# Two blocks of a feed-forward layer share one PSUM bank, and weight steps may be issued while the tensor engine waits

## The chip, the cores and the metric

The kernel runs on one core of a Trainium2 chip. Time is device time in microseconds (us) of the whole launch, as the median of several runs. Engines are named as the profile names them: PE is the tensor engine (PEld its loading of stationary operands), DVE the vector engine, ACT the scalar engine, POOL the GpSimd engine, SP the queue that issues most transfers.

## The reference

```python
# attention: q, k, v are (8, 8, 576, 64); 64-wide blocks, a query sees its own block and earlier ones
scores = scale * np.matmul(q, k.transpose(0, 1, 3, 2))
mask = block_i >= block_j
attn = softmax(np.where(mask, scores, -1e9))
x = (attn @ v).transpose(0, 2, 1, 3).reshape(8, 576, 512)
# Fourier mixing and a feed-forward net
mixed = np.real(np.fft.fft(np.fft.fft(x, axis=1), axis=2))
u = x + mixed
un = (u - mean(u)) / np.sqrt(var(u) + 1e-6)             # per row of 512
ch = np.maximum(un @ w_ch1, 0.0) @ w_ch2                 # 512 -> 2048 -> 512
return u + ch
```

## The kernel before

There are 64 heads (8 batches of 8). The heads run as attention with exact maxima: `max_part` (line 392 reduces), `shift`, `scores` (two exponentials on ACT, lines 434 and 435, and a difference `pl` on POOL, line 436), `values` (matmuls into `av`). Each operand is held as a high and a low part. After eight heads of a batch, `fourier_steps` reads the batch back mirrored (`mirror`: two plain loads by SP and three gathers by POOL, line 538), folds it on DVE (lines 549 and 550), and multiplies it with cosine and sine tables (`stage1`, `stage2_sin`, `stage2_cos`). `normalized_steps` normalizes 256 rows (`norm`, line 694) and transposes them on PE (`turn`, line 705 casts, line 706 takes the low part). Each such group of 256 rows becomes one feed; there are 18 feeds.

A feed (`feed_steps`) has 16 blocks f of 128 hidden columns. `first(f, part)` issues 3 of the 12 matmuls (256 columns each) that build a block in a PSUM tile `h`; behind the last part ACT writes `gh` = relu of it (line 743) and DVE the rest `gl` (line 744). `second(f, n)` issues 3 of the 6 matmuls (512 columns each) that multiply `gh` and `gl` with the second weights into the two tiles `acc`. The order is first(0), first(1), second(0), first(2), second(1), and so on. The pool `h` has two banks; each tile is a bank, of which a block fills half.

What stands where is set by a planner in the program itself. Lanes (loads, preparation, v, maxima, scores, values, transforms) hold steps with estimated costs, `after` (keys that must be done in the estimate) and `need` (keys that must have been issued). The loop at the end of the kernel issues the ready step of the lowest `place`; feed steps are the filler, issued where no lane is ready. A further stream, the weight steps (`weight_lane`: `weight_single` packs the 64-bit weights of the input with three DVE operations, lines 823 to 825, and squares them on ACT, line 826; `weight_parts` makes the two fp16 parts on ACT, lines 850 and 853, and on POOL, line 854, or DVE, line 856), is the `side`. A side step was issued only if it was ready at the estimated present:

```python
if side is not None and may(side) and ready(side) <= now:
    engine, cost = side.chain[0]
    ahead = queues[engine].fit(max(now, ready(side)), cost) - now
```

PE keeps the program's order. On the other engines a scheduler places instructions as their operands allow, and each engine then works strictly through its own list.

Of the kernel before, what the change touches and what calls it, by code (L numbers as in the profile page):

```python
# [9 lines left out]
F32 = mybir.dt.float32  # L10
F32R = mybir.dt.float32r
F16 = mybir.dt.float16
# [7 lines left out]
B, H, S, D = 8, 8, 576, 64  # L20
DM = H * D
FF = 4 * DM
P = 128
NF = FF // P
NK = DM // P
# [10 lines left out]
AHEAD = (1.5, 6.0)  # L36
FREE = 0.5
# [141 lines left out]
def tile_attn_fourier_ffn(  # L179
# [5 lines left out]
    work = pool("work")  # L185
    ps_av = pool("ps_av", 1, space=PSUM)
    ps = {name: pool(name, n, space=PSUM) for name, n in BANKS.items()}
# [5 lines left out]
    def mm(*args, **kw):  # L193
        return tc.keep_in_program_order(nc.tensor.matmul(*args, **kw))  # L194
# [43 lines left out]
    for at in range(0, NCOS, P):  # L238
        w = min(P, NCOS - at)
        nc.vector.tensor_scalar(ZT[:, at:at + w], ones[0:34, 0:w], 0.0, None, op0=ALU.mult)  # L240

    W = const.tile([P, 2 * NF + 2, 2, DM], F16, name="W")
# [4 lines left out]
    now = 0.0  # L247
    queues = {x: Queue() for x in "DAGQ"}
# [5 lines left out]
    def may(step):  # L254
        return all(x in done for x in step.after) and all(x in done for x in step.need)

    def ready(step):
        r = max((done[x] for x in step.after), default=0.0)
        return max(r, min(rings[x][0] for x in lent)) if step.bank else r

    def issue(step):
        nonlocal current, now
        t = max(now, ready(step))
        if step.cost:
            now = t = t + step.cost
            for x in queues.values():
                x.forget(now)
        free = None
        for engine, cost in step.chain:
            if engine == "B":  # L270
                free = t + HOP
            else:
                t = t + cost if engine == "L" else queues[engine].book(t + HOP, cost)
        t += HOP
        if step.key is not None:
            done[step.key] = t
        if step.bank:
            current = min(lent, key=lambda x: rings[x][0])
            rings[current] = rings[current][1:] + [t if free is None else free]
        step.emit()  # L280
# [444 lines left out]
    def feed_steps(me, uh, ul, us, stores):  # L725
        acc = []
        gs = {}

        def first(f, part):
            fs = slice(P * (f % NK), P * (f % NK + 1))  # L730
            if part == 0:
                gs[f] = ps["h"].tile([P, 512], F32, name="h")[:, 0:2 * P]
            t = gs[f]
            i = 3 * part
            for w, x_ in ((0, uh), (0, ul), (1, uh)):
                mm(t, W[:, NK * (f // NK) + part, w, fs], x_[:, part], start=(i == 0), stop=(i == 3 * NK - 1))
                i += 1
            if part < NK - 1:
                return
            gh = work.tile([P, 2 * P], F16, name="gh", bufs=3)  # L740
            gl = work.tile([P, 2 * P], F16, name="gl", bufs=3)
            gs[f] = gh, gl
            nc.scalar.activation(gh, t, AF.Relu)  # L743
            nc.vector.scalar_tensor_tensor(gl, t, 0.0, gh, op0=ALU.max, op1=ALU.subtract)  # L744

        def second(f, n):
            if f == 0:
                acc.append(ps["acc"].tile([P, DM], F32, name="acc"))
            gh, gl = gs[f]
            ns = slice(P * n, P * (n + 1))  # L750
            for j, (g_, w) in enumerate(((gh, 0), (gh, 1), (gl, 0))):
                mm(acc[n], g_[:, ns], W[:, NF + f, w], start=(f == 0 and j == 0), stop=(f == NF - 1 and j == 2))
            if f == NF - 1:
                u = us[n]
                nc.vector.scalar_tensor_tensor(u, acc[n], inv_w, u, op0=ALU.mult, op1=ALU.add)
                stores[n](u)

        def first_steps(f):
            for part in range(NK):
                last = part == NK - 1  # L760
                after = (("t", me, 0), ("t", me, 1)) + ((("g", me, f - 2),) if f > 1 else ()) if part == 0 else ()
                if me == 1:
                    after += (("w", NK * (f // NK) + part),)
                yield Step(
                    lambda part=part: first(f, part), 0.327, ("A0.4", "D0.44") if last else (), after,
                    ("g", me, f) if last else None,
                )

        def second_steps(f):
            for n in range(2):  # L770
                yield Step(
                    lambda n=n: second(f, n), 0.648, ("D0.76",) if f == NF - 1 else (), (("g", me, f),) + ((("w", NF + f),) if me == 1 else ()),
                    ("F", me) if f == NF - 1 and n == 1 else None,
                )

        yield from first_steps(0)
        for f in range(NF):
            if f + 1 < NF:
                yield from first_steps(f + 1)
            yield from second_steps(f)  # L780


    stage = [utile() for _ in range(3)]
# [74 lines left out]
    def weight_lane():  # L858
        yield Step(lambda: weight_loads(0), 0.0, ("Q5",), (("L", 0),), ("load",))
        def single(x):  # L860
            i, n, at = LANDS[x]
            return Step(
                lambda: weight_single(x), 0.0, (f"D{0.19 + 0.26 * n}", f"D{0.19 + 0.62 * n}", f"D{0.19 + 0.63 * n}", f"A{0.38 + 0.43 * n}"),
                (("load",),), "w32" if x == len(LANDS) - 1 else None,
            )

        def scale(w):
            return Step(lambda: weight_scale(w), 0.1, ("D0.16", "B", "D0.45"), (), ("scale", w), True)

        def parts(i):  # L870
            return Step(lambda: weight_parts(i), 0.0, ("A1.45", "G1.2") if i < NF else ("A0.73", "D0.75"), (("scale", i // NF),), ("w", i))

        for x in range(len(LANDS)):
            i, n, at = LANDS[x]
            yield single(x)
            if i == NF - 2:
                yield scale(0)
            if i >= NF:
                for j in range(n):
                    yield parts(i - NF + j)  # L880
        yield scale(1)
        for i in range(NF):
            yield parts(NF + i)
# [22 lines left out]
    heads = [next(x) for x in lanes]  # L906
    weights, filler = weight_lane(), None
    side = next(weights)
    while True:
        if filler is None and feeds:  # L910
            filler = next(feeds[0], None)
            if filler is None:
                feeds.pop(0)
                continue
        able = [
            i for i, x in enumerate(heads)
            if x is not None and may(x) and (i == len(lanes) - 1 or x.place < H or "w32" in done)
        ]
        if side is not None and may(side) and ready(side) <= now:
            engine, cost = side.chain[0]  # L920
            ahead = queues[engine].fit(max(now, ready(side)), cost) - now
            idle = min((ready(heads[i]) for i in able), default=now)
            if filler is not None and may(filler):
                idle = min(idle, ready(filler))
            if ahead <= AHEAD[engine == "D" and min((heads[i].place for i in able), default=H) >= H] or ahead + cost + FREE <= idle - now:
                issue(side)
                side = next(weights, None)
                continue
        feed = filler is not None and may(filler)
        sure = now - (MARGIN if feed and ready(filler) <= now else 0.0)  # L930
        soon = [i for i in able if ready(heads[i]) <= sure]
        if soon:
            i = min(soon, key=lambda i: heads[i].place)
        elif feed and ready(filler) <= now or feed and not able:
            i = None
        elif able:
            i = min(able, key=lambda i: ready(heads[i]))
        elif side is not None:
            issue(side)
            side = next(weights, None)  # L940
            continue
        else:
            assert filler is None and not any(heads)
            break
        if i is None:
            lent = ["ps"]
            issue(filler)
            filler = None
        else:
            issue(heads[i])  # L950
            heads[i] = next(lanes[i], None)
# [46 lines left out]
```

## Time and profile before

| what | value |
|---|---|
| median of 3 runs | 1330.21 us (1328.94 to 1335.06) |
| the profiled execution | 1334.54 us |
| its span, first to last instruction | 1332.8 us |
| PE busy | 1193.2 us (90%) |
| DVE, ACT, POOL busy | 53%, 43%, 40% |
| mean granted PE clock | 0.963 |

Busy time counts an engine's instructions; matmuls overlap, so a busy PE is not PE at its peak. The granted clock is given as a share of full speed: 1.00 is 2.4 GHz, 0.50 is 1.2 GHz, and a value between is a mean over the stretch.

### The profile page before, as it was taken

To read this page: it belongs to the slowest core of one execution; us is meant where nothing else is said; L and a number is where in the kernel's file an instruction comes from. 1 tells how busy PE (TensorE), PEld (TensorE's weight loads), DVE (VectorE), ACT (ScalarE), POOL (GpSimd) and SP (SyncE) were. 2 spreads that over 40 slices of the span, in tenths; PEclk is the share of its full clock that TensorE was granted. 3 is DMA by queue.
4 is the path that set the end of the run, shared out by engine and by line. 5 is a ranking of instruction groups with operands and counts; after the bars stand their busy time and mean duration, and the time that the engine had idled before them with its cause. 6 is when DMAs were issued, how large, how long until landed. Compare 5 with 4: busy or idle time off the path is not lost.

```text
span 1332.8 us, 25628 instructions
## 1 busy us (share of the span) xinstructions
PE 1193.2 (90%) x10068; PEld 892.8 (67%) x10068; DVE 702.9 (53%) x1584; ACT 567.2 (43%) x1281; POOL 533.1 (40%) x578
## 2 busy tenths in 40 slices
PE   2565379999999998999999998999999999999998
PEld 2455257767776776767777676777767667666665
DVE  6984687565646757564555654457433433312221
ACT  3569357544545555445545444454322212111111
POOL 4479244546544853654544474344600302100000
PEclk9997679989899999999999898999999999999999
DMA  9655313332332233234333223230011000000000
GB/s 281 218 154 176 108 32 83 99 91 60 82 103 76 61 85 105 59 80 108 94 80 96 65 60 90 75 96 25 21 32 34 23 17 21 17 1 17 16 17 16
DMA packets 55943, 99.10 MB, mean 74 GB/s; under 512 B 7709, under 2 KB 26605, under 8 KB 55696
## 3 DMA queue, kind: packets, MB, share of 16 engines
q1 hardware_dynamic: 52176, 87.56, 23.4%
q0 software_dynamic: 2288, 7.54, 1.9%
q10 hardware_dynamic: 1360, 2.38, 0.6%
q8 instruction: 79, 1.29, 0.4%
q14 instruction: 40, 0.33, 0.1%
HBM read 58.46 MB, written 18.87 MB: 58 GB/s over the span
## 4 chain that ended last, share of the span: by engine, by line
PE 71%; DVE 9%; POOL 4%; ACT 3%; issue 2%; DMA 2%; DVEq 0%; SPq 0%; POOLq 0%; ACTq 0%
PE h L194 25%; PE acc L194 25%; PE ps L194 14%; PE av L194 5%; POOL pl L436 2%; DVE tmp L549 2%; PE ps L197 1%; DVE M L392 1%; DMA U<-xd,rows 1%; DVE rest L308 1%; DVE tmp L550 1%; DVE fs L518 1%; DVE W L856 1%; DVE gl L744 1%; ACT lead L293 1%
## 5 line engine op out<-in xcount | busy, mean ns | idle before, releaser
L194 PE MATMUL h<-uh,W 128*128 128x256 f16 x2304 | 455.3, 276 | 0.0
L436 POOL TENSOR_TENSOR pl<-p,ph 128x288 f16<-128x288 f32 (+1 forms) x256 | 256.8, 1013 | 355.6 <-ACT p L435 229.6
L194 PEld LDWEIGHTS <-W 128*128 128x128 f16 x3456 | 325.4, 99 | 89.9 <-issue 5.4
L194 PE MATMUL acc<-W,gh 128*128 128x512 f16 x1152 | 348.6, 385 | 0.0
L194 PE MATMUL h<-ul,W 128*128 128x256 f16 x1152 | 316.7, 275 | 0.0
L744 DVE SCALAR_TENSOR_TENSOR gl<-h,gh 128x256 f16<-128x256 f32 x288 | 120.8, 420 | 294.2 <-ACT gh L743 292.5
L743 ACT ACTIVATE gh<-h 128x256 f16<-128x256 f32 x288 | 110.2, 383 | 369.1 <-PE h L194 358.6
L194 PE MATMUL acc<-W,gl 128*128 128x512 f16 x576 | 220.8, 383 | 5.3 <-DVE gl L744 5.2
L194 PE MATMUL ps<-lead 72*128 72x64 f32 (+9 forms) x696 | 198.4, 344 | 9.7 <-ACT lead L293 6.7
L434 ACT ACTIVATE ph<-ps 128x288 f16<-128x288 f32 (+1 forms) x236 | 119.7, 508 | 94.2 <-PE ps L194 92.8
L194 PE MATMUL av<-VH,pl 128*128 128x65 f16 x960 | 118.6, 202 | 38.8 <-POOL pl L436 36.9
L194 PEld LDWEIGHTS <-gh 128*128 128x128 f16 x1152 | 101.8, 99 | 65.6 <-issue 6.8
L392 DVE TENSOR_REDUCE M<-ps 128x1 f32<-128x320 f32 (+3 forms) x227 | 117.3, 531 | 43.1 <-PE ps L194 41.9
L194 PEld LDWEIGHTS <-ph 128*128 128x128 f16 x1920 | 114.6, 104 | 36.4 <-issue 12.3
L194 PEld LDWEIGHTS ps<-lead 73*128 73x128 f32 (+1 forms) x696 | 125.7, 200 | 19.0 <-ACT lead L293 6.7
L194 PE MATMUL av<-VH,ph 128*128 128x65 f16 x960 | 120.8, 203 | 14.7 <-DVE x L474 11.8
L194 PE MATMUL ps<-rest 128*128 128x64 f32 (+2 forms) x357 | 126.3, 360 | 4.0 <-DVE M L392 3.3
L310 POOL TENSOR_TENSOR rest<-raw,lead 64x576 fp32r<-64x576 f32 x64 | 117.8, 1840 | 24.7 <-ACT lead L293 19.3
L435 ACT ACTIVATE p<-ps 128x288 f32<-128x288 f32 (+1 forms) x236 | 119.5, 507 | 13.0 <-POOL pl L436 10.2
L194 PEld LDWEIGHTS <-pl 128*128 128x128 f16 x960 | 94.7, 103 | 42.4 <-POOL pl L436 40.3
L194 PE MATMUL av<-VL,ph 128*128 128x64 f16 x960 | 120.0, 201 | 0.0
L194 PEld LDWEIGHTS <-gl 128*128 128x128 f16 x576 | 56.8, 99 | 77.8 <-DVE gl L744 9.5
(171 smaller groups left out, 1393.7 us busy)
## 6 DMA issues: line engine op xcount, KB each, us to landing
raw<-in_qk_dram SPq DMA_DIRECT2D x64, 288.0 KB
rest<-lead SPq DMA_DIRECT2D x112, 144.0 KB
W<-in_moe_w_ch_dram SPq DMA_DIRECT2D x14, 1024.0 KB
V<-in_v_dram SPq DMA_DIRECT2D x32, 320.0 KB
xd<-x SPq DMA_DIRECT2D x32, 256.0 KB
out_dram<-u SPq DMA_DIRECT2D x32, 256.0 KB
u<-xd SPq DMA_DIRECT2D x8, 512.0 KB
dft<-in_c_dft_dram POOLq DMA_DIRECT2D x1, 2606.0 KB
```

What stands on the lines that cost most here:

```text
L194: return tc.keep_in_program_order(nc.tensor.matmul(*args, **kw))
L197: return tc.keep_in_program_order(nc.tensor.transpose(*args, **kw))
L293: nc.scalar.copy(LEAD[h % NB][0:D, 64:], raws[h])
L308: nc.vector.tensor_tensor(x0[0:D, 0:S], raw[:, 0:S], x1[0:D, 64:64 + S], op=ALU.subtract)
L310: nc.gpsimd.tensor_tensor(x0[D:P, S:], raw[:, S:], x1[0:D, 64 + S:], op=ALU.subtract)
L392: nc.vector.tensor_reduce(m[:, j:j + 1], t[:, at - hi:at], axis=AX.X, op=ALU.max)
L434: nc.scalar.activation(ph[:, at:at + w], t[:, 0:w], AF.Exp, scale=0.125)
L435: nc.scalar.activation(p32[:, 0:w], t[:, 0:w], AF.Exp, scale=0.125)
L436: nc.gpsimd.tensor_tensor(pl[:, at:at + w], p32[:, 0:w], ph[:, at:at + w], op=ALU.subtract)
L549: nc.vector.tensor_tensor(e[0:r], X[c][0:r], U[c][0:r], op=op)
L743: nc.scalar.activation(gh, t, AF.Relu)
L744: nc.vector.scalar_tensor_tensor(gl, t, 0.0, gh, op0=ALU.max, op1=ALU.subtract)
```

## The change

Two blocks 2k and 2k+1 of a feed now fill the two halves of one bank. The bank is opened by the first matmul of the even block and closed by the last of the odd one; one ACT operation over 512 columns writes `gh` for both, and one DVE operation `gl` (two buffers of double width in place of three). The order becomes first(0), first(1), first(2), first(3), second(0), second(1), first(4), first(5), second(2), second(3), and so on. In the planner a weight step may now be issued if it will be ready by the time at which the next lane or filler step can run (`until`), so also in an estimated wait of PE.

```diff
-            if part == 0:
-                gs[f] = ps["h"].tile([P, 512], F32, name="h")[:, 0:2 * P]
-            t = gs[f]
+            if f % 2 == 0 and part == 0:
+                gs[f] = ps["h"].tile([P, 512], F32, name="h")
+            t = gs[f - f % 2]
+            half = t[:, 2 * P * (f % 2):2 * P * (f % 2 + 1)]
...
-                mm(t, W[:, NK * (f // NK) + part, w, fs], x_[:, part], start=(i == 0), stop=(i == 3 * NK - 1))
+                mm(
+                    half, W[:, NK * (f // NK) + part, w, fs], x_[:, part], start=(f % 2 == 0 and i == 0),
+                    stop=(f % 2 == 1 and i == 3 * NK - 1), skip_group_check=True,
+                )
...
-            gh = work.tile([P, 2 * P], F16, name="gh", bufs=3)
-            gl = work.tile([P, 2 * P], F16, name="gl", bufs=3)
-            gs[f] = gh, gl
+            gh = work.tile([P, 4 * P], F16, name="gh", bufs=2)
+            gl = work.tile([P, 4 * P], F16, name="gl", bufs=2)
+            for x in range(2):
+                gs[f - 1 + x] = (gh[:, 2 * P * x:2 * P * (x + 1)], gl[:, 2 * P * x:2 * P * (x + 1)])
...
-                after = (("t", me, 0), ("t", me, 1)) + ((("g", me, f - 2),) if f > 1 else ()) if part == 0 else ()
+                if part == 0 and f % 2 == 0:
+                    after = (("t", me, 0), ("t", me, 1)) + ((("g", me, f - 4),) if f > 3 else ())
...
         yield from first_steps(0)
-        for f in range(NF):
-            if f + 1 < NF:
-                yield from first_steps(f + 1)
-            yield from second_steps(f)
+        yield from first_steps(1)
+        for f in range(0, NF, 2):
+            for steps in (first_steps, second_steps):
+                for x in range(2):
+                    if steps is second_steps:
+                        yield from steps(f + x)
+                    elif f + 2 < NF:
+                        yield from steps(f + 2 + x)
...
-        if side is not None and may(side) and ready(side) <= now:
-            engine, cost = side.chain[0]
-            ahead = queues[engine].fit(max(now, ready(side)), cost) - now
-            idle = min((ready(heads[i]) for i in able), default=now)
-            if filler is not None and may(filler):
-                idle = min(idle, ready(filler))
-            if ahead <= AHEAD[engine == "D" and min((heads[i].place for i in able), default=H) >= H] or ahead + cost + FREE <= idle - now:
+
+        until = [ready(heads[i]) for i in able] + ([ready(filler)] if filler is not None and may(filler) else [])
+        until = max(now, min(until, default=now))
+        if side is not None and may(side) and ready(side) <= until:
+            engine, cost = side.chain[0] if side.chain else (None, 0.0)
+            at = max(now, ready(side))
+            ahead = queues[engine].fit(at, cost) - at if engine else 0.0
+            first = min((heads[i].place for i in able), default=H) >= H
+            if ahead <= AHEAD[engine == "D" and first] or at + ahead + cost + FREE <= until:
```

The change also moves much of the order. Three places follow.

The first is ACT in batch 0, where the parts of the first weights begin (lines 850 and 853 before, 863 and 866 of the changed file; `ph` and `p` are the two exponentials of a head, `lead` its operand copy). Before:

```order
L435 ACTIVATE p_836<-acc 128x288
L302 DMA rest_88<-lead_85 64x576
L434 ACTIVATE ph_855<-acc 128x512
L435 ACTIVATE p_862<-acc 128x512
L339 ACTIVATE VH_95<-V,vacc 128x10x64
L850 ACTIVATE W<-W,wst 128x512
L853 ACTIVATE un<-W,wst 128x512
```

And after:

```order
L435 ACTIVATE p_862<-acc 128x512
L434 ACTIVATE ph_892<-ps 128x512
L293 CAST lead_86<-raw 64x1152
L435 ACTIVATE p_899<-ps 128x512
L434 ACTIVATE ph_960<-h 128x288
L863 ACTIVATE W<-W,wst 128x512
L866 ACTIVATE un<-W,wst 128x512
```

The parts began inside head 5 (counted from 0) and now begin inside head 6. Ahead of the last exponential of head 7 stand 17 of these operations where 21 stood, and on POOL 8 of line 854 where 10 stood.

The second is POOL at the gathers of batch 5 (line 538) among the differences `pl` of the heads (line 436) and the operand copies (line 310). Before:

```order
L436 TENSOR_TENSOR pl_11192<-p_11203,ph_11191 128x288
L436 TENSOR_TENSOR pl_11215<-p_11221,ph_11214 128x512
L436 TENSOR_TENSOR pl_11236<-p_11242,ph_11235 128x512
L310 TENSOR_TENSOR rest_89<-raw,lead_86 64x576
L538 DMA u<-xd,rows 128x512 x2
L436 TENSOR_TENSOR pl_11398<-p_11402,ph_11397 128x288
L436 TENSOR_TENSOR pl_11398<-p_11419,ph_11397 128x288
```

And after:

```order
L436 TENSOR_TENSOR pl_10380<-p_10384,ph_10379 128x288
L436 TENSOR_TENSOR pl_10380<-p_10396,ph_10379 128x288
L538 DMA u<-xd,rows 128x512 x2
L538 DMA U_11177<-xd,rows 32x512
L436 TENSOR_TENSOR pl_10414<-p_10420,ph_10413 128x512
L436 TENSOR_TENSOR pl_10425<-p_10431,ph_10424 128x512
```

The two gathers into `u` stood ahead of both differences of a head's first chunk; now that chunk's differences stand ahead of them.

The third is PE behind the last transform matmul of batch 1 (`ps<-dft,ZT`). Before:

```order
L194 MATMUL ps<-dft,ZT 128x258
L194 MATMUL ps<-lead_86 128x64 x2
L194 MATMUL ps<-lead_86 128x192
L194 MATMUL ps<-lead_86 128x320
L194 LDWEIGHTS W
L194 MATMUL h<-uh,W 128x256
```

And after:

```order
L194 MATMUL ps<-dft,ZT 128x258
L194 MATMUL ps<-vacc,ones 128x1
L197 MATMUL ps<-ident,M_91 5x128
L194 MATMUL ps<-lead_86 128x64 x2
L194 MATMUL ps<-lead_86 128x192
L194 MATMUL ps<-lead_86 128x320
L194 MATMUL ps<-lead_86 128x448
L194 MATMUL ps<-lead_86 128x512
L194 MATMUL ps<-rest_88 128x288
L194 MATMUL ps<-lead_85 128x288
```

Before, steps of batch 0's second feed (`h<-uh,W`) followed at once. Now that feed is used up earlier, and two heads' maxima, scores and values alone stand between the transform and the transposes of batch 1.

## Rows read from the trace of the kernel before

**Rows 1.** The page: busy time of PE, and the granted clock in 40 slices.
```profile
PE 1193.2 (90%) x10068; PEld 892.8 (67%) x10068; DVE 702.9 (53%) x1584; ACT 567.2 (43%) x1281; POOL 533.1 (40%) x578
...
PEclk9997679989899999999999898999999999999999
```

**Rows 2.** Stretches: length, then busy us of PE, PEld, DVE, ACT, POOL, granted clock, transfers.
```profile
22.00:86.00 64.00, 31.92 (x225) 27.48 (x226) 62.04 (x85) 35.59 (x73) 39.95 (x21) 1.00 0.73 227
...
102.00:132.00 30.00, 17.06 (x179) 14.73 (x178) 14.74 (x31) 28.28 (x53) 28.04 (x25) 0.77 0.59 182
132.00:155.00 23.00, 1.46 (x3) 0.79 (x3) 12.76 (x27) 7.50 (x17) 7.95 (x10) 0.50 0.44 156
155.00:186.00 31.00, 21.90 (x154) 18.27 (x155) 26.46 (x62) 12.63 (x30) 11.10 (x16) 0.77 0.10 24
186.00:966.00 780.00, 741.95 (x6882) 567.31 (x6883) 454.35 (x1082) 399.41 (x909) 396.08 (x420) 0.97 0.29 77
```

**Rows 3.** Waits of PE from 186 to 1333 us: total, times, longest.
```profile
PE av L194 <- POOL pl L436: 12.9, 11, 4.2
...
PE acc L194 <- DVE gl L744: 5.2, 5, 1.8
```

**Rows 4.** Four stretches of the middle, columns as in the second group.
```profile
336.00:356.00 20.00, 17.32 (x141) 13.22 (x139) 14.38 (x33) 9.60 (x22) 10.08 (x11) 0.83 0.35 101
...
738.00:754.00 16.00, 13.14 (x109) 9.97 (x108) 9.98 (x22) 6.22 (x15) 4.68 (x6) 0.79 0.08 20
...
812.00:834.00 22.00, 16.81 (x124) 11.98 (x122) 9.14 (x23) 8.20 (x18) 7.63 (x8) 0.77 0.33 95
...
902.00:916.00 14.00, 11.06 (x100) 8.02 (x98) 13.30 (x25) 8.25 (x19) 5.25 (x6) 0.88 0.10 22
```

**Rows 5.** Groups by shape: count, busy us, mean ns of one, idle before.
```profile
L743 ACT ACTIVATE gh<-h 128x256 f16<-128x256 f32 x288 | 110.2, 383 | 369.1 <-PE h L194 358.6 <-DVE vacc L333 5.0 <-PE ps L194 3.4
L434 ACT ACTIVATE ph<-ps 128x512 f16<-128x512 f32 x121 | 72.5, 600 | 33.3 <-PE ps L194 32.1
...
L744 DVE SCALAR_TENSOR_TENSOR gl<-h,gh 128x256 f16<-128x256 f32 x288 | 120.8, 420 | 294.2 <-ACT gh L743 292.5 <-issue 1.2
...
L755 DVE SCALAR_TENSOR_TENSOR u<-acc,inv_w,u 128x512 f32<-128x512 f32 x32 | 23.0, 745 | 11.8 <-PE acc L194 11.8
...
L850 ACT ACTIVATE W<-W,wst 128x512 f16<-128x512 f32 x32 | 22.1, 714 | 4.6 <-DVE W L856 4.5
...
L854 POOL TENSOR_TENSOR W<-un,W 128x512 f16<-128x512 f32 x16 | 18.3, 1158 | 5.0 <-ACT un L853 4.7
```

**Rows 6.** Order of time around 818 us, POOL and PE: start, us, instruction, [idle before].
```profile
818.47 1.11 POOL L538 DMA_INDIRECT u<-xd,rows  x1 [7.33 <-DMA out_dram<-u]
...
820.92 1.41 POOL L436 TENSOR_TENSOR pl<-p,ph 128x288 f16<-128x288 f32 x2
...
821.70 0.24 PE L194 MATMUL av<-VH,pl 128*128 128x65 f16 x1 [4.23 <-POOL pl L436]
```

**Rows 7.** Batch 1 from its last transform matmul to its transposes.
```profile
326.70 0.38 PE L194 MATMUL ps<-dft,ZT 34*128 34x258 f32 x1
...
335.92 0.55 DVE L694 TENSOR_SCALAR un<-u,ag 128x512 f32<-128x512 f32 x1 [0.47 <-POOL ag L692]
...
346.17 0.60 PE L197 MATMUL ps<-ident,un 128*128 128x128 f32 x4
```

**Rows 8.** DVE and PE at 975 us.
```profile
975.53 0.69 DVE L549 TENSOR_TENSOR tmp<-u 128x512 f32<-128x512 f32 x1 [1.39 <-DMA u<-xd,rows]
976.14 0.42 DVE L744 SCALAR_TENSOR_TENSOR gl<-h,gh 128x256 f16<-128x256 f32 x1
...
976.62 0.39 PE L194 MATMUL acc<-W,gl 128*128 128x512 f16 x1 [1.82 <-DVE gl L744]
```

**Rows 9.** Two evictions in a row on ACT near the end.
```profile
1297.03 0.38 ACT L743 ACTIVATE gh<-h 128x256 f16<-128x256 f32 x1 [2.22 <-PE h L194]
...
1299.64 0.38 ACT L743 ACTIVATE gh<-h 128x256 f16<-128x256 f32 x1 [2.22 <-PE h L194]
```

More of the change, by code (lines that the diff above doesn't have):

```diff
@@ L730, in first @@
             fs = slice(P * (f % NK), P * (f % NK + 1))
-            if part == 0:
-                gs[f] = ps["h"].tile([P, 512], F32, name="h")[:, 0:2 * P]
-            t = gs[f]
+            if f % 2 == 0 and part == 0:
+                gs[f] = ps["h"].tile([P, 512], F32, name="h")
+            t = gs[f - f % 2]
+            half = t[:, 2 * P * (f % 2):2 * P * (f % 2 + 1)]
             i = 3 * part
             for w, x_ in ((0, uh), (0, ul), (1, uh)):
-                mm(t, W[:, NK * (f // NK) + part, w, fs], x_[:, part], start=(i == 0), stop=(i == 3 * NK - 1))
+                mm(
+                    half, W[:, NK * (f // NK) + part, w, fs], x_[:, part], start=(f % 2 == 0 and i == 0),
+                    stop=(f % 2 == 1 and i == 3 * NK - 1), skip_group_check=True,
+                )
                 i += 1
-            if part < NK - 1:
+            if f % 2 == 0 or part < NK - 1:
                 return
-            gh = work.tile([P, 2 * P], F16, name="gh", bufs=3)
-            gl = work.tile([P, 2 * P], F16, name="gl", bufs=3)
-            gs[f] = gh, gl
+            gh = work.tile([P, 4 * P], F16, name="gh", bufs=2)
+            gl = work.tile([P, 4 * P], F16, name="gl", bufs=2)
+            for x in range(2):
+                gs[f - 1 + x] = (gh[:, 2 * P * x:2 * P * (x + 1)], gl[:, 2 * P * x:2 * P * (x + 1)])
             nc.scalar.activation(gh, t, AF.Relu)
@@ L759, in first_steps @@
             for part in range(NK):
-                last = part == NK - 1
-                after = (("t", me, 0), ("t", me, 1)) + ((("g", me, f - 2),) if f > 1 else ()) if part == 0 else ()
+                last = f % 2 == 1 and part == NK - 1
+                after = ()
+                if part == 0 and f % 2 == 0:
+                    after = (("t", me, 0), ("t", me, 1)) + ((("g", me, f - 4),) if f > 3 else ())
                 if me == 1:
@@ L764, in first_steps @@
                 yield Step(
-                    lambda part=part: first(f, part), 0.327, ("A0.4", "D0.44") if last else (), after,
-                    ("g", me, f) if last else None,
+                    lambda part=part: first(f, part), 0.327, ("A0.6", "D0.72") if last else (), after,
+                    ("g", me, f - 1) if last else None,
                 )
@@ L771, in second_steps @@
                 yield Step(
-                    lambda n=n: second(f, n), 0.648, ("D0.76",) if f == NF - 1 else (), (("g", me, f),) + ((("w", NF + f),) if me == 1 else ()),
+                    lambda n=n: second(f, n), 0.648, ("D0.76",) if f == NF - 1 else (),
+                    (("g", me, f - f % 2),) + ((("w", NF + f),) if me == 1 else ()),
                     ("F", me) if f == NF - 1 and n == 1 else None,
```

## Prediction

> **What bounds the kernel now.** I read the page first: PE is busy 1193.2 us of a span of 1332.8, far above the others [rows 1]. Then I cut the span into stretches. From 22 to 86 us DVE is the bound (62.04 of 64 us busy), from 102 to 132 us ACT and POOL are (28.28 and 28.04 of 30), from 132 to 155 us almost nothing runs on PE (1.46 of 23) and the clock stands at its lower level, and from 155 to 186 us batch 0's transform ends [rows 2]. Only behind that do feeds fill PE: of the 780 us from 186 to 966, 741.95 are busy, at a mean granted clock of 0.97 [rows 2].
>
> So the time is PE's work plus what PE waits plus what the lower clock costs. I count a loss in a stretch as length minus busy time, plus (1 − granted clock) × length. Four stretches of the middle carry much of it: 2.7 + 3.4 = 6.1 us at 336–356, 2.9 + 3.4 at 738–754, 5.2 + 5.1 at 812–834, 2.9 + 1.7 at 902–916 [rows 4].
>
> Third came PE's waits by releaser: 12.9 us for `pl`, the difference on POOL, and 5.2 us in five waits for `gl`, one of them 1.8 us [rows 3]. Fourth, the order of time at two of these. At 976 us `gl` starts only when a fold of line 549 before it on DVE has gone through, and PE's next matmul of `acc` waits 1.82 us for it [rows 8]. At 818 us POOL stands 7.33 us at a gather that waits for a store, `pl` comes behind it at 820.92, and PE waits 4.23 us [rows 6]. Where nothing disturbs it, a block takes 1299.64 − 1297.03 = 2.61 us from one eviction to the next [rows 9]; its 12 matmuls of 256 columns and 6 of 512 are 6144 columns, so 0.42 ns per column.
>
> **The change part by part.**
>
> *Evictions.* 288 of 0.383 us on ACT become 144 of 512 columns. That shape of `gh` isn't in the trace; the nearest is an exponential of 128x512 at 0.600 us [rows 5], so 144 × 0.600 = 86 in place of 110.2 us. On DVE 288 × 0.420 = 121 become 144 × 0.745 (the row of line 755, three operands, 512 columns) = 107. ACT had 369.1 us of idle time before these, nearly all of it waiting for PE [rows 5]: the saving lies off the path and I cost it at nothing. If that cover were gone, the 14 to 24 us would still be spread over some 1150 us, a gain.
>
> *PE's matmuls.* Same count, same columns: zero.
>
> *Slack of `gl`.* Before, 2.6 us of PE work (one block) usually stands between the last `first` of a block and its `second`. Now the odd block's `gl`, which comes 0.2 us + 0.3 us later by the longer operations, has two `second` blocks of the pair before it: at least 5.2 us, except at 14 places at feeds' ends (2.6). The longest wait was 1.8 beyond 2.6 us [rows 3], so 5.2 + 0.5 us later covers it. I take the five waits as gone: −5.2 us (0 to −5.2). They stand partly in 738–754 and 902–916, and their lower clock (3.4 + 1.7 us, [rows 4]) follows the bursts. I take half: −2.5 us (0 to −5.1).
>
> *The two buffers in place of three.* Second(p) now stands ahead of first(p + 2) on PE, so the eviction of a pair finds its buffer free; hidden by the matmuls of a pair, 5.2 us. Zero; if it weren't, each of 144 pairs would show a wait of ACT for PE.
>
> *Start.* The weight steps begin one head later: ahead of head 7's last exponential stand 17 operations of 0.714 us on ACT where 21 stood, and 8 of 1.158 us on POOL where 10 stood [rows 5]. That is −2.9 on ACT, −2.3 on POOL, in a stretch where these two are the bound. I take −2.4 us (0, if DVE or a store paces, to −6, with the clock at 0.77 given back). The parts that moved behind lie in the hole of 132–155, where ACT is busy 7.50 of 23 us and POOL 7.95 [rows 2].
>
> *POOL's gathers of batch 5.* In the new order the first chunk's two `pl` stand ahead of the gathers, and the next `values` that need POOL come after 2 to 5 us of other PE work. The stretch lost 10.3 us. I expect most of it back but charge 2 us because batch 6's gathers now fall between two halves of a `pl` with 2.6 us of PE work behind: −6 us (0 to −10.1).
>
> *Batch 1.* This is what the change takes away. Before, steps of batch 0's second feed followed the last transform matmul, so PE had work for the norm of batch 1. After, both feeds of batch 0 are used up earlier, and between that matmul and the transposes stand 12 maxima and 12 score matmuls (6400 columns, 2.7 us at 0.42 ns), 15 matmuls of `values` and 3 small transposes: 3.3 us with 0.04 us each for these, 5.6 with the 0.19 us of an isolated short matmul; I take 4.5. The chain beside it runs from 326.70 + 0.38 to the end of the second `un` at 335.92 + 0.55: 9.4 us [rows 7]. PE therefore idles some 4.9 us there. The row 336–356 shows what such waits do to the clock: 0.83, 3.4 us in 20 [rows 4]. With about 3 more for the heads' own chain (maxima, shift, scores with nothing between), the stretch costs 4.9 + 3.4 + 2.8 = 11.1 and gives back its own 6.1 [rows 4]: +5 us (+2 if the folds end earlier for want of `gl`; +15 if the clock also stands at 0.50 through the 16.6 us of PE work that this stretch then holds, as in 132–155 [rows 2]: 4.9 + 16.6 − 6.1). The Trainium skill, "TensorE: Matmul & The Clock Gate", section "HAM oscillation — how this bites in real kernels", says that waits between bursts of matmuls put the array back to half rate, and that what it costs goes by the share of time so throttled. The row agrees in kind: 0.83 and not 1.00 in a stretch with 2.7 us of waits. [...]
>
> Sum: −2.4 − 5.2 − 2.5 − 6 + 5 = −11.1 us against the profiled 1334.54, so 1323.4 there. That execution lies 4.3 us above the median of 1330.21; against the median the forecast is **1319 us**.
>
> **The rivals.**
>
> *The middle isn't won (first rival).* DVE's fold bursts and POOL's gathers aren't shortened by the change, only met by other PE work: a wait that goes at 738 and 818 may come back at another batch, and with it the clock. For it: PE's waits for `pl` are eleven, not one, and the longest, 4.2 of 12.9 us, is the only one whose neighbours I followed [rows 3]. Against it: the same order took the cover from batch 5's gather and would have to take it again elsewhere. Then −2.4 − 5.2 + 5 = −2.6: 1327.6 us, no measurable difference.
>
> *Batch 1 runs like the end of batch 0 (second rival, slower).* From transform to transposes no feed is left. The 16.6 us of PE work in it (scores, the transform's end, values, transposes) are my estimate: columns at 0.42 ns, four times that for 32-bit operands. At the pace of 155–186 (21.90 busy of 31, [rows 2]) it would last 23.5 us, +6.9; at the clock of 132–155, 0.50 [rows 2], its work doubles, +16.6. Less the 6.1 it lost before, +17.4. With only the start and the `gl` waits won (−7.6) that is +9.8: 1340 us. It decides from about +14.3 us in that stretch, since 7.6 + 6.65 must be passed. Against it: the clock in 336–356 and in 155–186 was 0.83 and 0.77, not 0.50, and heads' work runs there too.
>
> *The weight steps gain nothing (third rival).* The condition lets a step out earlier, but in the new order the parts stand later than before and the start may be paced by loads or by DVE (62.04 of 64 us in 22–86, [rows 2]). Then the −2.4 is gone: 1321.4 us.
>
> **How the numbers follow.** Chances: the forecast 0.52, first rival 0.24, second 0.16, third 0.08. A measurement of this kernel tells about 0.5% (6.65 us) from no change, so faster means below 1323.6, slower above 1336.9. The forecast and the third rival lie below (0.58; of the forecast's spread 0.02 falls in between); the first is mostly between (0.20) with 0.03 below and 0.01 above; the second above: 0.6, 0.23, 0.17. Low end: all gains at their bounds and batch 1 at +2, that is −6 − 5.2 − 5.1 − 10.1 + 2 = −24.4, 1306. High end: up to 1336, past the first rival and below the second's, which leaves some 0.16 above. The forecast's own range is 1311 to 1326.
>
> **What would show it.** Right: 144 evictions of line 743's kind at about 0.6 us; PE's wait for `gl` near zero; no gather on POOL ahead of a `pl` for which PE waits over 4 us; the last exponential of head 7 some 2.4 us earlier, and the first feed with it; PE's busy time in the last 360 us as before. Batch 1's stretch, from its last transform matmul to its transposes, shows 8 to 14 us of loss. Wrong: a clock near 0.5 there for 15 us or more (second rival), or a granted clock of 0.97 or less and as much idle time in the middle as before at other batches (first rival). The prediction also fails if 512-column evictions take far more than 0.75 us and the odd block's `gl` comes late, or if the first feed starts later than at 186 us because more weight work now stands on DVE ahead of batch 0's transform.

## The result and the profile after

The changed kernel takes 1315.51 us (median of 4 runs, 1311.42 to 1316.90) against 1329.58 us before: a ratio of 0.988, 95% interval 0.9859 to 0.9901. The forecast was 1319 us, in a range of 1306 to 1336. The profiled execution took 1315.5 us, its span is 1313.7 us, 19.1 us less than that of the profiled execution before (which lay above its median).

The page of the changed kernel, to hold against [rows 1]:

```profile
PE 1184.2 (90%) x10068; PEld 886.7 (67%) x10068; DVE 671.9 (51%) x1440; ACT 548.5 (42%) x1137; POOL 530.0 (40%) x578
...
PEclk9955679999699999999999999999999999999999
```

PE does the same 10068 matmuls; DVE and ACT have 144 instructions fewer each and are 31.0 and 18.7 us less busy. The clock shows one dip in the middle, in the 11th slice (about 328 to 361 us).

The stretches of the changed kernel (columns as in [rows 2]):

```profile
22.00:86.00 64.00, 30.36 (x250) 26.18 (x251) 62.53 (x87) 36.39 (x74) 39.86 (x21) 0.87 0.74 233
102.00:132.00 30.00, 12.31 (x126) 10.38 (x122) 9.49 (x22) 26.61 (x49) 26.66 (x24) 0.52 0.58 160
132.00:155.00 23.00, 7.35 (x27) 5.49 (x28) 16.80 (x35) 8.18 (x22) 5.03 (x7) 0.52 0.32 117
...
320.00:400.00 80.00, 72.71 (x628) 55.58 (x626) 42.89 (x96) 37.28 (x76) 42.58 (x50) 0.87 0.26 68
400.00:480.00 80.00, 75.96 (x683) 57.47 (x680) 49.88 (x112) 35.55 (x80) 42.63 (x53) 0.98 0.29 81
480.00:966.00 486.00, 472.15 (x4383) 359.92 (x4381) 267.70 (x616) 236.79 (x501) 238.22 (x255) 1.00 0.29 79
```

The same three late stretches of the kernel before:

```profile
320.00:400.00 80.00, 77.32 (x700) 59.39 (x699) 45.26 (x112) 40.66 (x91) 45.40 (x52) 0.96 0.33 88
400.00:480.00 80.00, 76.67 (x721) 59.61 (x719) 53.78 (x127) 40.09 (x94) 47.46 (x55) 0.98 0.26 70
480.00:966.00 486.00, 460.74 (x4286) 351.36 (x4285) 271.75 (x653) 239.38 (x550) 239.66 (x257) 0.97 0.29 76
```

With a loss counted as in the prediction (length minus busy, plus (1 − clock) × length), three numbers tell the result. From 480 to 966 us the loss falls from 25.3 + 14.6 = 39.9 us to 13.9 + 0 = 13.9 us: 26 us won. From 320 to 400 us, batch 1's transform, it rises from 2.7 + 3.2 = 5.9 to 7.3 + 10.4 = 17.7 us: 11.8 us lost. And the first feed starts 5.7 us earlier. First the changed kernel, then the kernel before:

```profile
180.50 0.44 PE L194 MATMUL h<-uh,W 128*128 128x256 f16 x1
```

```profile
186.19 0.28 PE L194 MATMUL h<-uh,W 128*128 128x256 f16 x1
```

−26 + 11.8 − 5.7 = −19.9 us, against spans that differ by 19.1; the other stretches add some −1 us between them, and the two digits of the clock leave some 2 us open in a stretch of 486. The profiled run of the kernel before lies 5 us above its median, so between the medians there is that much less to divide.

PE's waits of the changed kernel from 186 to 1314 us, against [rows 3] (total, times, longest):

```profile
PE av L194 <- POOL pl L436: 16.6, 14, 2.1
...
PE ps L197 <- DVE M L394: 3.9, 4, 1.5
PE ps L194 <- ACT tmp L323: 2.6, 2, 2.0
PE ps L194 <- DVE ul L706: 2.2, 3, 1.3
...
PE acc L194 <- DVE gl L750: 0.4, 1, 0.4
```

The waits for `gl` are gone (5.2 to 0.4 us). Those for POOL's `pl` are more, not fewer, but the longest is 2.1 us where it was 4.2. The evictions by shape, against [rows 5]:

```profile
L750 DVE SCALAR_TENSOR_TENSOR gl<-h,gh 128x512 f16<-128x512 f32 x144 | 98.9, 687 | 227.3 <-ACT gh L749 227.2
L749 ACT ACTIVATE gh<-h 128x512 f16<-128x512 f32 x144 | 85.9, 596 | 268.4 <-PE h L194 267.7
```

0.596 us on ACT (0.600 forecast) and 0.687 on DVE (0.745 forecast).

Batch 1's stretch, its loss and its path (to hold against [rows 7]):

```profile
329.00:351.00 22.00, 16.09 (x98) 12.12 (x98) 18.07 (x44) 7.95 (x18) 15.36 (x24) 0.64 0.24 59
329.68:345.34 15.66, 13.09 (x70) 9.70 (x69) 12.31 (x32) 6.34 (x14) 13.79 (x23) 0.56 0.17 44
```

```profile
329.68 0.38 PE L194 MATMUL ps<-dft,ZT 34*128 34x258 f32 x1
...
331.94 1.43 PE L194 MATMUL ps<-lead 72*128 72x448 f32 x2 [0.56 <-DVE M L392]
334.50 0.61 PE L194 MATMUL ps<-rest 128*128 128x288 f32 x1 [1.12 <-DVE M L392]
...
338.38 0.76 PE L194 MATMUL ps<-lead 72*128 72x512 f32 x1 [0.59 <-DVE M L392]
...
342.03 0.41 PE L197 MATMUL ps<-ident,M 128*5 128x128 f32 x1
342.34 1.12 PE L197 MATMUL ps<-ident,un 128*128 128x128 f32 x4
...
344.24 1.10 PE L197 MATMUL ps<-ident,un 128*128 128x128 f32 x4
...
347.66 0.38 PE L194 MATMUL ps<-lead 72*128 72x320 f32 x1 [1.30 <-DVE ul L706]
...
350.07 0.59 PE L194 MATMUL ps<-vacc,ones 128*128 128x1 f32 x2 [2.03 <-ACT tmp L323]
```

The second `un`, on DVE:

```profile
340.13 0.54 DVE L694 TENSOR_SCALAR un<-u,ag 128x512 f32<-128x512 f32 x1
```

In these 22 us PE lacks 5.9 us and runs at a mean clock of 0.64, so 5.9 + 7.9 = 13.8 us are lost. None of the idle time is a wait for the norm. The second `un` is done at 340.67, and PE comes to the transposes only at 342.34, without idle time before them. Ahead of them it waits 2.3 us, each time for `M`, the maxima of a head; behind them it waits 3.3 us more, for `ul` and for a head's `tmp`. What lasted is PE's work: from the last transform matmul to the end of the transposes PE is busy 13.09 us at a mean clock of 0.56.

### The profile page after: what moved, and what is told of

Read it like the earlier page. It is cut to its first block, busy times and chain, and to the rows that moved or that the text cites. A ratio compares the mean times of both kernels' runs of the same rounds, so it can differ in the third digit from the quotient of the medians.

```text
span 1313.7 us, 25264 instructions
## 1 busy us (share of the span) xinstructions
PE 1184.2 (90%) x10068; PEld 886.7 (67%) x10068; DVE 671.9 (51%) x1440; ACT 548.5 (42%) x1137; POOL 530.0 (40%) x578
## 4 chain that ended last, share of the span: by engine, by line
PE 76%; DVE 10%; ACT 4%; DMA 3%; POOL 3%; issue 3%; SPq 0%; ACTq 0%; DVEq 0%; POOLq 0%
PE h L194 27%; PE acc L194 26%; PE ps L194 16%; PE av L194 5%; POOL pl L436 2%; PE ps L197 1%; DVE M L392 1%; DVE W L837 1%; DMA W<-in_moe_w_ch_dram 1%; DVE rest L308 1%; DVE W L838 1%; ACT lead L293 1%; DVE tmp L549 1%; DMA U<-xd,rows 1%; DVE W L836 1%
## 5 line engine op out<-in xcount | busy, mean ns | idle before, releaser
L194 PE MATMUL h<-uh,W 128*128 128x256 f16 x2304 | 434.9, 275 | 0.0
L750 DVE SCALAR_TENSOR_TENSOR gl<-h,gh 128x512 f16<-128x512 f32 x144 | 98.9, 687 | 227.3 <-ACT gh L749 227.2
L749 ACT ACTIVATE gh<-h 128x512 f16<-128x512 f32 x144 | 85.9, 596 | 268.4 <-PE h L194 267.7
L434 ACT ACTIVATE ph<-ps 128x512 f16<-128x512 f32 (+1 forms) x229 | 116.0, 507 | 121.0 <-PE ps L194 119.7
L392 DVE TENSOR_REDUCE M<-ps 128x1 f32<-128x320 f32 (+3 forms) x235 | 120.5, 527 | 47.9 <-PE ps L194 46.7
L194 PEld LDWEIGHTS ps<-lead 72*128 72x128 f32 (+1 forms) x700 | 125.6, 201 | 20.8 <-ACT lead L293 6.8
L310 POOL TENSOR_TENSOR rest<-raw,lead 64x576 fp32r<-64x576 f32 x64 | 116.2, 1816 | 23.3 <-ACT lead L293 18.5
L194 PE MATMUL av<-VH,ph 128*128 128x65 f16 x960 | 118.1, 202 | 8.2 <-DVE x L474 7.6
L194 PE MATMUL ps<-rest 128*128 128x64 f32 (+2 forms) x345 | 121.6, 360 | 1.8 <-DVE M L392 1.1
L435 ACT ACTIVATE p<-ps 128x512 f32<-128x512 f32 (+1 forms) x229 | 115.9, 506 | 10.2 <-POOL pl L436 10.1
L308 DVE TENSOR_TENSOR rest<-raw,lead 64x576 fp32r<-64x576 f32 x64 | 60.0, 938 | 88.4 <-ACT lead L293 88.3
```

Of the source, the lines that this page charges most:

```text
L308: nc.vector.tensor_tensor(x0[0:D, 0:S], raw[:, 0:S], x1[0:D, 64:64 + S], op=ALU.subtract)
L310: nc.gpsimd.tensor_tensor(x0[D:P, S:], raw[:, S:], x1[0:D, 64 + S:], op=ALU.subtract)
L392: nc.vector.tensor_reduce(m[:, j:j + 1], t[:, at - hi:at], axis=AX.X, op=ALU.max)
L434: nc.scalar.activation(ph[:, at:at + w], t[:, 0:w], AF.Exp, scale=0.125)
L435: nc.scalar.activation(p32[:, 0:w], t[:, 0:w], AF.Exp, scale=0.125)
```

## The experiments

Ratios are to the kernel before, run on the same chip; each has its 95% interval.

| kernel | order of the steps | feeds | ratio | interval |
|---|---|---|---|---|
| changed kernel | new | pairs | 0.988 | 0.9859 to 0.9901 |
| rule_only | of its own | blocks | 0.9972 | 0.9958 to 0.9986 |
| pair_only | of its own | pairs | 0.9909 | 0.9887 to 0.9931 |
| old_feed_new_order | new | blocks | 1.0055 | 1.0034 to 1.0076 |
| pair_old_order | before | pairs | 1.0003 | 0.9986 to 1.002 |
| pair_rule_order | of rule_only | pairs | 0.9961 | 0.9944 to 0.9979 |
| one_by_one | new | PE as pairs, a bank for each block | 1.0015 | 1.0000 to 1.0029 |
| halves | new | pairs, halves evicted apart | 0.9918 | 0.9901 to 0.9936 |
| spliced | of rule_only, then new | pairs | 0.9801 | 0.9780 to 0.9823 |
| gather_moved | before | blocks | 0.9945 | 0.9925 to 0.9965 |
| gather_moved_pairs | before | pairs | 0.9929 | 0.9904 to 0.9953 |
| splice_late | of rule_only, then new | pairs | 0.9815 | 0.9785 to 0.9845 |

**The two parts apart.** The first kernel has only the last part of the diff (`until`), the second all but this.

> Only the rule for the weight steps is changed; feeds run block by block as before. Theory (the two parts are separate): the first feed starts near 180.5 us as in the changed kernel instead of 186.2, batch 1's transform stays covered by feed steps because blocks are used up as late as before, PE's waits for gl stay near 5 us: 1323 to 1327 us. Rival (the rule alone carries the gain, the pairs add nothing): 1318 us or less.

> Only the pairs; weight steps by the old rule. Theory: the first feed starts at 186 us as before, PE's wait for gl is below 1 us, feeds of batch 0 are used up early and batch 1's transform loses 15 to 20 us instead of 6, and the middle behind 480 us loses some 15 us less than before: 1318 to 1323 us. Rival (the pairs' loss at batch 1 eats their gain): 1327 us or more.

Measured: 0.9972 and 0.9909; of the 1329.58 us before, these are 1325.9 and 1317.5 us, the second half a microsecond below its range. The theory holds for both: the first feed starts at 181.8 and 186.1 us, `gl` is waited for 3.3 us in `rule_only` and not at all in `pair_only`, and the 80 us from 320 on lose 4.8 and 18.5 us. The parts multiply to 0.9881, the 0.988 of the whole. The rule alone is worth 0.28%, 3.7 us. The program's order agrees: up to its 286th step (the first feed begins at the 278th) the order depends on the rule alone, and behind it the feeds alone part the kernels. `pair_only` uses up batch 0's two feeds when 86 steps of `values` have been issued, the changed kernel at 90, `before` and `rule_only` at 100 and 101: the early use comes with the pairs.

**Order and feed apart.** The planner's loop is replaced by the list of its decisions, one character for each step, so that any order can be given to either kind of feed:

```diff
-    while True:
...
+    ORDER = (
...
+    for x in ORDER:
+        if x == "s":
...
             issue(side)
             side = next(weights, None)
...
+        elif x == "f":
+            while filler is None:
+                filler = next(feeds[0], None)
...
             issue(filler)
             filler = None
         else:
+            i = int(x)
...
             issue(heads[i])
             heads[i] = next(lanes[i], None)
```

> All steps of heads, transforms and weights, and the slots of the feed steps, stand exactly as in the changed kernel; but in these slots feeds 2 to 18 run block by block in the old order with old evictions (feed 1 stays in pairs). Theory (the order of everything else makes most of the gain, the pairs' own slack only the waits for gl): those waits come back, 4 to 8 us, batch 1's loss stays: 1319 to 1323 us. Rival (the pairs' slack is the gain): 1327 us or more.

> All other steps and the slots of the feed steps stand exactly as in the kernel before; in these slots the feeds run in pairs. Theory one (sharing a bank gives slack, and that alone is worth the waits for gl and a part of their clock; the 4.2 us wait behind the gather of batch 5 stays): 5 to 8 us faster than before. Theory two (most of the gain is in the pairs' slack wherever they stand): 11 us or more faster than before. Rival (the order must be made for pairs): no change.

> The order is that of the kernel with the weight rule alone, in which batch 1 keeps its feed steps; the feeds run in pairs. Theory one: the 3.7 us of the rule and the 5 to 8 us of the pairs add up: 9 to 12 us faster than before, slower than the changed kernel by 3 to 6 us. Theory two: 15 us or more faster than before.

Measured: 1.0055, 1.0003, 0.9961. My theory fell in all three. The new order with the old feeds is slower than the kernel before; pairs in the old order gain nothing, and in the order of `rule_only` they add 0.11%, within the intervals. Beside the 0.3% of the rule, neither the pairs nor the order made for them is worth anything by itself; the rest of the 1.2% needs both.

Why do the pairs gain nothing in the old order, though `gl` is no longer waited for? PE's waits of `pair_old_order`:

```profile
PE av L194 <- POOL pl L436: 15.2, 13, 4.5
PE ps L194 <- DVE M L392: 7.7, 8, 2.8
PE av L194 <- DVE x L474: 5.3, 3, 3.4
PE ps L194 <- DVE fs L518: 1.6, 3, 1.1
```

`gl` is off the list, and the others have grown: `pl` from 12.9 to 15.2 [rows 3], `x` to 5.3. One place shows it. In the kernel before, at 742 us:

```profile
742.50 0.39 PE L194 MATMUL acc<-W,gl 128*128 128x512 f16 x1 [1.71 <-DVE gl L744]
...
745.22 0.24 PE L194 MATMUL av<-VH,ph 128*128 128x65 f16 x1 [1.15 <-DVE M L394]
```

In `pair_old_order`, at the same step:

```profile
743.46 0.24 PE L194 MATMUL av<-VH,ph 128*128 128x65 f16 x1 [3.37 <-DVE x L474]
```

There the 1.71 us that PE no longer waits for `gl`, it waits for `x` of a head, behind the same folds on DVE: 2.86 us in two waits became 3.37 us in one. A feed that doesn't wait only comes sooner to the head's step that does.

**Bank or number of evictions.** Both kernels keep PE's order of the changed kernel step by step. In the first each block has a bank of its own, as before:

```diff
-            if f % 2 == 0 and part == 0:
-                gs[f] = ps["h"].tile([P, 512], F32, name="h")
-            t = gs[f - f % 2]
-            half = t[:, 2 * P * (f % 2):2 * P * (f % 2 + 1)]
+            if part == 0:
+                gs[f] = ps["h"].tile([P, 512], F32, name="h")[:, 0:2 * P]
+            half = t = gs[f]
...
-            if f % 2 == 0 or part < NK - 1:
+            if part < NK - 1:
```

In the second the shared bank stays, but each half is evicted by operations of its own:

```diff
-            nc.scalar.activation(gh, t, AF.Relu)
-            nc.vector.scalar_tensor_tensor(gl, t, 0.0, gh, op0=ALU.max, op1=ALU.subtract)
+            for x in range(2):
+                xs = slice(2 * P * x, 2 * P * (x + 1))
+                nc.scalar.activation(gh[:, xs], t[:, xs], AF.Relu)
+                nc.vector.scalar_tensor_tensor(gl[:, xs], t[:, xs], 0.0, gh[:, xs], op0=ALU.max, op1=ALU.subtract)
```

> PE's order is exactly that of the changed kernel, but each block has its own bank and is evicted alone, 288 operations of 256 columns each on ACT and DVE. Theory (the fewer, longer evictions lie off the path; PE's order is what counts): 1313 to 1318 us, with ACT and DVE some 20 to 25 us busier each. Rival (the time that the evictions free on DVE and ACT shortens the heads' chains): 1321 us or more.

> The changed kernel, but the two halves of the shared bank are evicted by two operations of 256 columns on ACT and two on DVE, one after the other, when the pair is complete: PE's order and the two banks with two blocks each stay. Theory (the shared bank, which lets four blocks lie in two banks, is what counts, and not the number of evictions): no wait of PE's h for gl, within 0.4 per cent of the changed kernel. Rival (the 23 us of ACT and DVE that single evictions cost each are what made the kernel with a bank for each block slow): 10 us or more slower than the changed kernel.

Measured: 1.0015 and 0.9918. The expectation for `one_by_one` was wrong by some 15 us, and not by the mechanism that its rival named, since `halves` has the same 288 evictions. PE's waits of `one_by_one` tell what it is:

```profile
PE av L194 <- POOL pl L436: 20.2, 14, 3.4
PE h L194 <- DVE gl L750: 9.6, 6, 3.8
```

and its longest wait, on PE, with the eviction that ends it, on DVE:

```profile
427.30 0.37 PE L194 MATMUL h<-uh,W 128*128 128x256 f16 x1 [3.83 <-DVE gl L750]
```

```profile
425.44 0.67 DVE L549 TENSOR_TENSOR tmp<-u 128x512 f32<-128x512 f32 x1
426.04 0.87 DVE L340 SCALAR_TENSOR_TENSOR VL<-V,vacc,VH 128x640 f16<-128x640 f32 x1
426.83 0.41 DVE L750 SCALAR_TENSOR_TENSOR gl<-h,gh 128x256 f16<-128x256 f32 x1
```

It is `first` that waits, because both banks still hold blocks whose `gl` stands behind the folds. With two blocks in a bank, that wait doesn't exist in the changed kernel's list. So what the pairs give is room: four blocks in two banks, which lets PE go on with feeds through a fold burst. The six waits are 9.6 of the some 18 us between this kernel and the changed one; single blocks with four banks were not run. Evicting the halves apart costs 0.38% between the two medians of ratios, some 5 us; the intervals (0.9859 to 0.9901, 0.9901 to 0.9936) only just meet. In `halves` ACT and DVE are 20.0 and 21.7 us busier than in the changed kernel.

**Batch 1.** Up to the start of the third feed the order of `rule_only`, in which batch 1 keeps its feed steps, from there that of the changed kernel.

> The changed kernel in another order: up to the start of the third feed that of the kernel with the weight rule alone, from there that of the changed kernel. Theory (the loss at batch 1, some 17 us against 6, comes from feed steps used up early, and nothing is given back for it later): batch 1 loses 6 to 8 us, 1304 to 1309 us. Rival (heads that the changed kernel brought forward there are missing later): 1312 us or more.

Measured: 1302.9 us, 0.9801, 1 us below the range of the theory, which holds; this version beats both kernels. Two stretches of it:

```profile
320.00:400.00 80.00, 76.16 (x698) 56.84 (x696) 41.01 (x91) 38.48 (x80) 38.95 (x46) 1.00 0.27 73
...
480.00:966.00 486.00, 473.80 (x4380) 361.06 (x4380) 271.73 (x623) 237.40 (x505) 239.73 (x256) 1.00 0.29 79
```

At batch 1 3.8 us are lost in place of 17.7, and the middle keeps its gain (12.2 us lost, 13.9 in the changed kernel). Nothing is given back for the feeds used up early.

**The gathers of batch 5.** One thing is moved: POOL's two gathers into `u` stand behind the two `pl` of the next head's first chunk, by an edge of issue order; no other engine's order changes in the first kernel; in the second a few rows of DVE, SP and POOL move with it.

```diff
-                nc.gpsimd.indirect_dma_start(
-                    dst, None, xd, bass.IndirectOffsetOnAxis(ap=rows[0:dst.shape[0], i:i + 1], axis=0)
-                )
+                with tc.issue_after(last_pl[217]) if b == 5 and i < 2 else ExitStack():
+                    nc.gpsimd.indirect_dma_start(
+                        dst, None, xd, bass.IndirectOffsetOnAxis(ap=rows[0:dst.shape[0], i:i + 1], axis=0)
+                    )
```

> The kernel before, with one thing moved: POOL's two gathers of batch 5 into u stand behind the two differences pl of the next head's first chunk, no longer ahead of them; every other engine's order is unchanged. Theory (the loss at 812 to 834 us comes from that place and is free to be won, the prediction's term of 6 us): PE's wait of 4.2 us for pl goes with its clock, 5 to 10 us faster than before. Rival (another wait of that head takes its place): within 3 us of before.

> The same move in the kernel with pairs in the old order, which was as fast as the kernel before and had a wait of 4.5 us for pl. Theory: 5 to 10 us faster than before. Rival: within 3 us of before; then neither the waits for gl nor this one are what the changed kernel's gain is made of.

Measured: 0.9945 and 0.9929, 7.3 and 9.5 us. Here a wait was free to be won. The stretch of `gather_moved`, against the third of [rows 4]:

```profile
812.00:834.00 22.00, 19.88 (x191) 14.77 (x190) 12.12 (x28) 11.65 (x27) 12.80 (x13) 1.00 0.30 87
```

The loss falls from 10.3 to 2.1 us, 8.2 us, 5.1 of them the clock, which stays at its upper level when the wait of 4.2 us is gone.

**Where in the middle the new order saves.** The splice of above, but at the start of the seventh feed.

> The changed kernel in another order: up to the start of the seventh feed that of the kernel with the weight rule alone, from there that of the changed kernel. Theory (the new order saves in the middle because heads and feeds stay side by side all the way; where heads have run ahead in the old order, that is lost): the losses of the old order up to the seventh feed stay, 1310 to 1318 us. Rival (the gain lies behind the seventh feed alone): 1302 to 1306 us.

Measured: 1308.6 us, between the two expectations; but the kernel before took 1332.5 us beside it, and 0.9815 of 1329.58 us are 1305 us, in the range of the rival. The interval overlaps nearly all of that of `spliced` and does not tell the two apart. It is 1.5% faster than `pair_rule_order`, whose order it shares up to there, so most of the gain of the new order lies behind the start of the seventh feed. Some 7 of these 19 us may be the gathers of batch 5, behind which `pair_rule_order` still waits 4.0 us for `pl`.

## Why the prediction was right, and where by luck

**Total and sign: right, in good part by luck.** Forecast −11.1 us on the profiled run, measured −14 between the medians (−19 between the profiled runs). Two steps failed, the waits for `gl` and the wait for the norm at batch 1. Two gains were more than twice as large as forecast, the start and the middle. The errors ran in opposite directions: no 7.7 us for `gl`, a batch 1 some 7 us dearer than the +5, against a middle that gained 26 us.

**The waits for `gl` (−5.2, and −2.5 for their clock): the step failed.** They vanished as forecast, and in the old order that was worth nothing: with the same order and no wait for `gl`, `pair_old_order` measures 1.0003 (0.9986 to 1.002). The step took a wait's length for its price. PE meets the next step that hangs on the same burst of DVE, and waits there. That is the mechanism which the first rival told of; it holds for this term, though not for the whole.

**The middle beyond that: mis-sized.** Forecast were −6 us, for the gathers; 480 to 966 us gained 26 us. `gather_moved` bears out the term of 6 us with 7.3 us (0.9925 to 0.9965). What the prediction put no price on is that pairs change what the planner may plan: by the program a new block may now begin when the block four before it is evicted, not two, so the plan spends feeds where it spent heads. At the start of the ninth feed the order of `rule_only` has issued 33 steps of `values` more than the new one, 6.6 heads. That the heads so kept back are the cover for the middle's later transforms fits this and the result of `splice_late`, but no run shows it by itself; besides the gathers' 7 us, the 26 us are not settled place by place.

**Batch 1 (+5): the step failed, the sign and the bounds held.** That the missing feed steps make this place dearer is shown by `spliced`: with cover the stretch loses 3.8 us. The 80 us from 320 on lost 11.8 us more than before, inside the bounds of +2 to +15. But the step said that PE idles 4.9 us for the norm, because 4.5 us of PE work stand beside a chain of 9.4 (the bounds of that work, 3.3 and 5.6 us, leave out the 3 transposes; with them they are 3.4 and 6.1). The chain took 10.6 us (from 329.68 + 0.38 to 340.13 + 0.54), and PE did not wait for it at all: the work beside it kept PE until 342.34, at the lower clock. That the idle time, 5.9 us, looks like the forecast is luck. It is 2.3 us for heads' maxima (the prediction had 2.8 for the heads' own chain) and 3.3 us behind the transposes, which the sum did not have. The other error is the clock, 0.64 over 22 us in place of the 0.83 of [rows 4].

Here the second rival had the better mechanism, PE work at the lower clock with no feed left: it named a clock near 0.5 for 15 us as its sign, and the 15.66 us to the end of the transposes ran at 0.56. Its price (+17.4) is about as far from the 11.8 us as mine. Its 16.6 us of PE work are too much: the 13.09 us busy at 0.56 are some 7.3 us at the full clock. It took four times 0.42 ns for a 32-bit column, 1.7 ns. In the kernel before, six matmuls of 258 such columns take 0.96 us together, 0.62 ns per column:

```profile
325.81 0.96 PE L194 MATMUL ps<-dft,zc 128*128 128x258 f32 x6
```

The second rival did not decide, since the middle gained 26 us and not 0.

**Start (−2.4): mechanism right, mis-sized.** Head 7's last exponential, in the changed kernel and in the kernel before:

```profile
120.63 0.57 ACT L435 ACTIVATE p<-h 128x512 f32<-128x512 f32 x1
```

```profile
126.87 0.57 ACT L435 ACTIVATE p<-ps 128x512 f32<-128x512 f32 x1
```

It comes 6.2 us earlier, and the first feed starts 5.7 us earlier, near the bound of −6. The counted operations are worth 2.3 to 2.9 us of this; where the rest comes from, no run shows. `rule_only` as a whole measures −3.7 us (1.9 to 5.6). Two kernels that share the old start, with the same 689 matmuls in the same order up to the first feed, show that the clock was no bound there. First `gather_moved`, then `pair_old_order`:

```profile
86.00:132.00 46.00, 31.23 (x292) 27.53 (x289) 24.90 (x51) 38.28 (x75) 37.12 (x33) 0.57 0.50 148
185.52 0.44 PE L194 MATMUL h<-uh,W 128*128 128x256 f16 x1
```

```profile
86.00:132.00 46.00, 32.99 (x294) 29.25 (x291) 24.61 (x51) 38.10 (x74) 36.23 (x33) 0.93 0.49 148
185.99 0.28 PE L194 MATMUL h<-uh,W 128*128 128x256 f16 x1
```

At a clock of 0.57 the first feed starts no later than at 0.93, so there was nothing to win from "the clock at 0.77 given back".

**Evictions (0): nearly right.** The 20 us of ACT and DVE lie off the path but for some 5 us (`halves`), at the edge of what the measurement tells. As cover the prediction named ACT's idle time, which is a mean over the feeds; inside fold bursts DVE has none.

**The banks: missed.** The prediction looked at buffers for `gh` and `gl` and at the slack of `second`, not at `first`, which has to find an empty bank. In the new order that is what single-block banks fail at (9.6 us in six waits).

## What to carry to other kernels

Price a wait by what is late next, not by its length: if the next step of the same engine hangs on the same burst, the wait only moves. When buffers grow, ask what the planner or the order will do with the room; measure order and buffer apart by replaying a fixed list of steps, for each may be worth nothing alone. And where filler work is spent earlier, look for the place that it used to cover: an order spliced from two plans came to 0.9801, the whole change to 0.988.

## What the runs showed of the hardware

The lower clock cost nothing where PE was not the bound: from 86 to 132 us, with the same instructions before it, the first feed started at 185.52 us after a mean clock of 0.57 and at 185.99 after 0.93. Where PE was the bound, the clock cost about as much as the idle time or more, by the count of (1 − clock) × length: 7.9 us beside 5.9 us at batch 1, and 5.1 us beside 5.2 us at 812–834 before the gathers were moved. That count takes in the idle time too, so it is an upper figure; at 812–834 it fell by 5.1 + 3.1 us, and the kernel measured 7.3 us less.
